# Loading the second token tile from GpSimd's queue, and transposing the first two tiles ahead of the first FFN product

## The chip, the cores and the metric

The kernel runs on one core of a Trainium2 chip. The metric is the device time of one execution in microseconds (us). The engines are named as in the profile: PE is TensorE, ACT is ScalarE, DVE is VectorE, POOL is GpSimd, SP is SyncE, which here only issues DMAs.

## What is computed

The input x has 2048 tokens of 640 features (bf16). It is normalised per token, then goes into two branches: linear attention with 32 heads of 20 features, and a two-layer FFN with 1728 hidden features. The output is x + s * g.

```python
xn = layernorm(x)                       # over the 640 features
q, k, v = split(xn @ wqkv)              # 32 heads
pq, pk = phi(q), phi(k)                 # phi(t) = t+1 if t > 0 else exp(t), plus 1e-6
o = (pq @ (pk.T @ v)) / (pq . sum(pk) + 1e-6)     # per head
s = o @ wo
g = silu(relu(xn @ w1) @ w2)
out = x + s * g
```

## The kernel before

The order of the work is written out by hand. A small recorder (`Sched`) takes each operation with the engine it is to run on, adds the semaphore waits that its reads and writes call for, and emits for each engine its instructions in the order of the calls. So each engine works through its own list in order, and an instruction that waits holds everything behind it on that engine. DMAs stand in the list of the engine that issues them.

Tokens are handled in 16 tiles of 128. The features of a tile are 5 chunks of 128. The FFN's first product and the query product work on groups of four tiles (512 tokens). The change lies in the start, where the first four tiles are brought in:

- `x_load(t)` (L334) loads tile t of x, 128 rows of 1280 bytes, into one of eight slots. `w1_load(i)` (L362) loads one of four column pieces of w1: columns 0 to 383, 384 to 639, 640 to 1151 and 1152 to 1727. `w_load` (L338) loads the key columns of wqkv ("wk"), the query columns ("wq") and others. L368 to L373 issue x0, x1, x2, the second piece of w1 and x3 from SP, and the first piece of w1 from ACT.
- L344 to L350 are POOL's first instructions: constants, among them `ident`, the identity that the transposes need.
- `fill` (L354) runs products of constants on PE into bank 0, whose results nobody reads.
- For tiles 0 to 3, `T_mean(t)` (L418) forms the mean of each token, on DVE or ACT, `center` (L430) subtracts it on DVE, `T_pe` (L435) transposes the chunks on PE into a PSUM bank, and `T_copy` (L440) copies them from there to `xnT`, on ACT or DVE. The division by the standard deviation comes later, in the scales of other operations.
- `H_first(t, fs, ks)` (L578) forms, for tile t alone, the first FFN product of the hidden blocks `fs` over the feature chunks `ks`, each block in a PSUM bank of its own (2 to 6); tile 3's call also evicts the blocks through a ReLU on ACT (`H_ev`). Blocks 0 to 2 need the first piece of w1, 3 and 4 the second.
- `LN_stats` (L392) forms mean and variance for the scales. From L688 on the key products (`K_mm`, L458) alternate with the other hidden blocks (`H_block`, L555); block 5 is the first reader of w1's third piece.

L584 to L626 order the start: nine fillers; tile 0's mean, centring, transposes and copies; 15 products of tile 0; then tile 1's mean, centring, transposes and copies; and so on through tile 3. A call `center(...)` returns a mark, kept as `held`, for which the next weight load waits on SP's queue.

Of the kernel before, what the change touches and what calls it, by code (L numbers as in the profile page):

```python
# [211 lines left out]
def bass_recurrent_scan__linear_attn_block__dense_activation_relu__prompt_kernel(  # L212
# [17 lines left out]
    C = D // P  # L230
# [92 lines left out]
    def dma(E, fn, R=(), W=(), extra=()):  # L323
        i = nds[0]
        nds[0] += 1
        return sc.dma(E, fn, i, R=R, W=W, extra=extra)

    def tok(t):
        return slice(P * t, P * (t + 1))
# [4 lines left out]
    def x_load(t, extra=(), E="SP"):  # L334
        sl = t % XR
        return dma(E, lambda eng: eng.dma_start(xin[:, sl, :], x2[tok(t), :]), W=[("xin", sl)], extra=extra)  # L336

    def w_load(dst, src, key, extra=(), E="SP"):  # L338
        dma(E, lambda eng: eng.dma_start(dst, src.rearrange("(c p) n -> p c n", p=P)), W=[key], extra=extra)


    cones = nc.const_aps.tensor(1.0, [P, P], bf)
    cwide = nc.const_aps.tensor(1.0, [P, 512], bf)
# [3 lines left out]
                                                fill=1.0, base=0, pattern=[[-1, P]], channel_multiplier=1),  # L347
# [6 lines left out]
    def fill(n, w=512):  # L354
        sc.group("PE", [(lambda eng: eng.matmul(ps[0][:, 0:w], lhsT=cones, rhs=cwide[:, 0:w], start=True, stop=True))
                        for _ in range(n)], W=[("ps", 0)])
# [5 lines left out]
    def w1_load(i, extra=(), E="SP"):  # L362
        w_load(w1_sb[:, :, W1C[i]:W1C[i + 1]], B_w1[:, W1C[i]:W1C[i + 1]], ("w1", i), extra, E)
# [3 lines left out]

    x_load(0)  # L368
    w1_load(0, E="ACT")
    x_load(1)  # L370
    x_load(2)
    w1_load(1)
    x_load(3)  # L373
# [18 lines left out]
    def LN_stats(t):  # L392
        xv = xin[:, t % XR, :]
        for a in range(2):
            sc.op("DVE", lambda eng, a=a: eng.bn_stats(stats[:, t, a, :], xv[:, HN * a:HN * (a + 1)]),  # L395
                  R=[("xin", t % XR)], W=[("stats", t, a)])
        sc.op("DVE", lambda eng: eng.bn_aggr(mv[:, t, :], stats[:, t, :, :].rearrange("p a b -> p (a b)")),
              R=[("stats", t, 0), ("stats", t, 1)], W=[("mv", t)])
        sc.op("POOL", lambda eng: eng.tensor_scalar(out=rsv[:, t:t + 1], in0=mv[:, t, 1:2], scalar1=EPS_LN,
                                                    scalar2=None, op0=ALU.add), R=[("mv", t)], W=[("rsv", t)])  # L400
        sc.op("POOL", lambda eng: eng.tensor_tensor(out=rsy[:, t:t + 1], in0=rsv[:, t:t + 1], in1=mhalf[:, :],
                                                    op=ALU.pow), R=[("rsv", t), ("mhalf",)], W=[("rsy", t)])
# [3 lines left out]
    def xnk(t, cs=range(C)):  # L406
        return [("xn", t, c) for c in cs]
# [10 lines left out]
    def T_mean(t, E="ACT"):  # L418
        if E == "ACT":
            sc.op("ACT", lambda eng: eng.activation(out=ek[:, 0, 0, :], in_=xin[:, t, :], func=ACTF.Copy, scale=1.0 / D,  # L420
                                                    accum_out=mean[:, t:t + 1]),
                  R=[("xin", t)], W=[("mean", t), ("ek_e", 0)])
        else:
            sc.op("DVE", lambda eng: eng.tensor_scalar(out=ek[:, 1, 0, :], in0=xin[:, t, :], scalar1=1.0 / D, scalar2=0.0,  # L424
                                                       op0=ALU.mult, op1=ALU.add, accum_out=mean[:, t:t + 1]),
                  R=[("xin", t)], W=[("mean", t), ("ek_e", 1)])
# [3 lines left out]
    def center(t, c0, c1):  # L430
        return sc.op("DVE", lambda eng: eng.tensor_scalar(
            out=xn[:, t, P * c0:P * c1], in0=xin[:, t, P * c0:P * c1], scalar1=mean[:, t:t + 1], scalar2=None,
            op0=ALU.subtract), R=[("xin", t), ("mean", t)], W=xnk(t, range(c0, c1)))

    def T_pe(t, c0, c1, b):  # L435
        psb = ps[b].bitcast(bf)
        sc.group("PE", [(lambda eng, c=c: eng.transpose(psb[:, P * c:P * (c + 1)], xn[:, t, P * c:P * (c + 1)], ident[:]))  # L437
                        for c in range(c0, c1)], R=xnk(t, range(c0, c1)) + [("ident",)], W=[("ps", b)])

    def T_copy(E, t, c0, c1, b):  # L440
        out = xnT[:, c0:c1, tok(t)]
        src = ps[b].bitcast(bf)[:, P * c0:P * c1].rearrange("p (c q) -> p c q", c=c1 - c0)
        if E == "ACT":
            sc.op("ACT", lambda eng: eng.activation(out=out, in_=src, func=ACTF.Copy), R=[("ps", b)],  # L444
                  W=xtk(t, range(c0, c1)))
        else:
            sc.op("DVE", lambda eng: eng.tensor_copy(out, src), R=[("ps", b)], W=xtk(t, range(c0, c1)))

    def xtk(t, cs=range(C)):
        return [("xnT", t, c) for c in cs]  # L450
# [93 lines left out]
    def H_mm(j, f, b, lo=0, hi=512, ks=range(C)):  # L544
        return sc.group("PE", [(lambda eng, k=k: eng.matmul(ps[b][:, lo:hi], lhsT=w1_sb[:, k, P * f:P * (f + 1)],  # L545
                                                            rhs=xnT[:, k, 512 * j + lo:512 * j + hi],
                                                            start=(k == 0), stop=(k == C - 1))) for k in ks],
                        R=[("w1", w1_part(f))] + [kk for q in range(lo // P, hi // P) for kk in xtk(4 * j + q, ks)],
                        W=[("ps", b)])

    def H_ev(j, f, b):
        sc.op("ACT", lambda eng: eng.activation(out=hT[:, f, schunk(j)], in_=ps[b], func=ACTF.Relu),  # L552
              R=[("ps", b)], W=[("hT", j, f)])
# [24 lines left out]
    def H_first(t, fs=range(5), ks=range(C)):  # L578
        for f in fs:
            H_mm(0, f, HF[f], P * t, P * t + P, ks)  # L580
            if t == 3:
                H_ev(0, f, HF[f])

    fill(9)  # L584
    T_mean(0, "DVE")
    center(0, 0, 2)
    T_pe(0, 0, 2, 7)
    held = center(0, 2, 5)
    T_pe(0, 2, 5, 1)
    T_copy("ACT", 0, 0, 2, 7)  # L590
    T_copy("DVE", 0, 2, 5, 1)
    w_load(wqk[:, :, D:2 * D], A_wqkv[:, D:2 * D], ("wk",), [held])
    fill(1, 192)
    H_first(0, (0, 1, 2), (0, 1))
    H_first(0, (0, 1, 2), (2, 3, 4))
    T_mean(1, "DVE")
    center(1, 0, 2)
    T_pe(1, 0, 2, 7)
    held = center(1, 2, 5)
    T_pe(1, 2, 5, 1)  # L600
    T_mean(2)
    T_copy("ACT", 1, 0, 2, 7)
    T_copy("DVE", 1, 2, 5, 1)
    w1_load(2, [held])
    x_load(4)
    x_load(5)
# [1 line left out]
    x_load(6)  # L608
    x_load(7)
    w_load(wqk[:, :, 0:D], A_wqkv[:, 0:D], ("wq",))  # L610
    H_first(0, (3, 4))
    T_mean(3)
    center(2, 0, C)
    H_first(1, (0, 1, 2, 3, 4), (0, 1))
    T_pe(2, 0, C, 7)
    T_copy("ACT", 2, 0, C, 7)
    center(3, 0, C)
    H_first(1, (0, 1, 2, 3, 4), (2, 3, 4))
    T_pe(3, 0, C, 1)
    T_copy("ACT", 3, 0, C, 1)  # L620
    LN_stats(0)
    LN_stats(1)
    LN_stats(2)
    LN_stats(3)
    H_first(2)
    H_first(3, (4, 0, 1, 2, 3))  # L626

    def z_split():
# [376 lines left out]
```

## Time and profile before

| | us |
|---|---|
| median of 3 runs | 222.18 (221.74 to 222.76) |
| the profiled execution | 222.18 |
| its span, from the first to the last instruction | 220.3 |
| PE busy | 215.1 (98%) |
| DVE busy | 115.1 (52%) |
| ACT busy | 87.5 (40%) |
| POOL busy | 43.5 (20%) |

The profile is of one execution. Times within it are us from the start of the span. A timeline row has start, duration, engine, line, operation, output<-input, and in brackets the engine's idle time ahead of it and what ended that. Instructions that are next to each other and alike are merged (x15). A row of a DMA issue (SPq, ACTq) is the time of issuing, not of the transfer; the transfer's end is seen where a reader starts, or in the views on DMA, which give the time from issue to landing. A DMA queue's row gives packets, MB, and the time of its packets as a share of all 16 engines'. `reg` stands for several buffers named reg1 to reg7, `psT` for all PSUM banks.

### The profile page before, as it was taken

To read this page: it belongs to the slowest core of one execution; us is meant where nothing else is said; L and a number is where in the kernel's file an instruction comes from. 1 tells how busy PE (TensorE), PEld (TensorE's weight loads), DVE (VectorE), ACT (ScalarE), POOL (GpSimd) and SP (SyncE) were. 2 spreads that over 40 slices of the span, in tenths; PEclk is the share of its full clock that TensorE was granted. 3 is DMA by queue.
4 is the path that set the end of the run, shared out by engine and by line. 5 is a ranking of instruction groups with operands and counts; after the bars stand their busy time and mean duration, and the time that the engine had idled before them with its cause. 6 is when DMAs were issued, how large, how long until landed. Compare 5 with 4: busy or idle time off the path is not lost.

```text
span 220.3 us, 3568 instructions
## 1 busy us (share of the span) xinstructions
PE 215.1 (98%) x1479; PEld 134.3 (61%) x1490; DVE 115.1 (52%) x198; ACT 87.5 (40%) x142; POOL 43.5 (20%) x66
## 2 busy tenths in 40 slices
PE   8899999999999999999999999999999999999994
PEld 2875554555545554444467778767767776777673
DVE  2878856789676999987700006603322222214053
ACT  3677775567656666555321114641021102110300
POOL 2153201269122997700000000000000000000001
PEclk9999999999999999999999999999999999999999
DMA  6995582213012105700069959368110100000002
GB/s 169 365 369 131 129 211 79 60 39 23 0 30 60 33 1 118 168 4 0 0 192 361 276 167 353 112 224 287 63 62 0 60 33 30 31 30 33 30 30 89
DMA packets 28812, 24.51 MB, mean 111 GB/s; under 512 B 11812, under 2 KB 28156, under 8 KB 28796
## 3 DMA queue, kind: packets, MB, share of 16 engines
q1 hardware_dynamic: 27996, 23.70, 37.1%
q10 hardware_dynamic: 800, 0.59, 1.0%
q8 instruction: 11, 0.18, 0.4%
q14 instruction: 5, 0.04, 0.1%
HBM read 15.75 MB, written 5.24 MB: 95 GB/s over the span
## 4 chain that ended last, share of the span: by engine, by line
PE 95%; DMA 2%; DVE 1%; issue 0%; SPq 0%
PE psT L845 26%; PE psT L545 25%; PE psT L891 10%; PE psT L462 10%; PE psT L790 10%; PE psT L530 10%; DMA reg<-in_A_x_dram 2%; PE psT L861 1%; PE psT L567 1%; PE psT L801 1%; PE psT L812 1%; PE psT L648 1%; PE psT L437 1%; DVE ek L424 0%; SPq L336 0%
## 5 line engine op out<-in xcount | busy, mean ns | idle before, releaser
L545 PE MATMUL psT<-reg 128*128 128x512 bf16 (+1 forms) x326 | 60.1, 330 | 0.8 <-ACT reg L444 0.2
L845 PE MATMUL psT<-reg,hT 128*128 128x320 bf16 x416 | 60.1, 299 | 0.0
L845 PEld LDWEIGHTS psT<-reg,hT 128*128 128x128 bf16 x416 | 40.4, 98 | 16.4 <-issue 1.1
L545 PEld LDWEIGHTS psT<-reg 128*128 128x128 bf16 x335 | 28.6, 98 | 25.9 <-issue 0.4
L913 DVE TENSOR_TENSOR reg<-psT,reg 128x640 bf16<-128x640 f32 x15 | 12.4, 825 | 54.0 <-PE psT L891 53.9
L552 ACT ACTIVATE hT<-psT 128x512 bf16<-128x512 f32 x52 | 30.7, 600 | 16.1 <-PE psT L545 16.0
L879 ACT ACTIVATE reg<-psT 128x640 bf16<-128x640 f32 (+1 forms) x13 | 8.4, 661 | 44.3 <-PE psT L845 24.9
L898 POOL TENSOR_TENSOR reg<-reg 128x256 bf16<-128x256 bf16 x1 | 0.7, 670 | 124.4 <-DVE reg L906 124.4
L530 PE MATMUL psT<-reg 128*128 128x512 bf16 x98 | 24.4, 379 | 0.1
L462 PE MATMUL psT<-reg 128*128 128x320 bf16 x160 | 24.2, 299 | 0.0
L471 POOL TENSOR_TENSOR zacc<-zacc,reg 128x640 f32<-128x640 f32 x16 | 23.7, 1484 | 1.9 <-DVE reg L505 1.0
L891 PE MATMUL psT<-reg,pqT 128*128 128x320 bf16 (+2 forms) x165 | 24.0, 295 | 0.0
L790 PE MATMUL psT<-reg 128*128 128x320 bf16 x160 | 21.9, 299 | 0.0
L462 PEld LDWEIGHTS psT<-reg 128*128 128x128 bf16 x160 | 15.6, 98 | 8.2
L891 PEld LDWEIGHTS psT<-reg,pqT 128*128 128x128 bf16 x165 | 16.0, 98 | 5.8
L790 PEld LDWEIGHTS psT<-reg 128*128 128x128 bf16 x160 | 15.7, 98 | 6.2
L540 DVE SCALAR_TENSOR_TENSOR pqT<-er 128x512 bf16<-128x512 bf16 x20 | 17.1, 854 | 0.7
L530 PEld LDWEIGHTS psT<-reg 128*128 128x128 bf16 x100 | 9.7, 98 | 11.7 <-DVE er L538 0.6
L537 ACT ACTIVATE er<-psT 128x512 bf16<-128x512 f32 x20 | 12.0, 598 | 8.9 <-PE psT L530 8.1
L538 DVE TENSOR_SCALAR er<-psT 128x512 bf16<-128x512 f32 x20 | 13.6, 679 | 3.1 <-ACT er L537 3.1
L505 DVE TENSOR_TENSOR reg<-ek 128x640 bf16<-128x640 bf16 x16 | 13.5, 843 | 1.5 <-ACT ek L496 1.0
L395 DVE BATCH_NORM_STATS2 stats<-reg 128x6 f32<-128x320 bf16 x32 | 13.9, 477 | 0.1
(63 smaller groups left out, 134.9 us busy)
## 6 DMA issues: line engine op xcount, KB each, us to landing
reg<-in_A_x_dram SPq DMA_DIRECT2D x16, 160.0 KB, 3.7
rscr<-rden SPq DMA_DIRECT2D x4, 640.0 KB, 11.1
reg<-rscr SPq DMA_DIRECT2D x5, 512.0 KB, 6.4
reg<-in_A_x_dram SPq DMA_DIRECT2D x4, 640.0 KB, 6.9
out_dram<-reg SPq DMA_DIRECT2D x15, 160.0 KB, 1.8
reg<-in_A_wqkv_dram SPq DMA_DIRECT2D x2, 800.0 KB, 7.3
reg<-in_B_w_dram SPq DMA_DIRECT2D x1, 1120.0 KB, 5.9
reg<-in_B_w_dram SPq DMA_DIRECT2D x1, 960.0 KB, 9.6
```

The costliest lines, as they stand in the source:

```text
L395: sc.op("DVE", lambda eng, a=a: eng.bn_stats(stats[:, t, a, :], xv[:, HN * a:HN * (a + 1)]), R=[("xin", t % XR)], W=[("stats", t, a)])
L462: fns.append(lambda eng, a=a, k=k: eng.matmul(ps[b + a][:, 0:HN], lhsT=xnT[:, k, tok(t)], rhs=wqk[:, k, D + HN * a:D + HN * (a + 1)], star ...
L471: sc.op("POOL", lambda eng: eng.tensor_tensor(out=zacc[:, :], in0=zacc[:, :], in1=pk[:, t, :], op=ALU.add), R=[("zacc",), ("pk", t)], W=[( ...
L505: sc.op("DVE", lambda eng: eng.tensor_tensor(out=pk[:, t, :], in0=e_, in1=r_, op=ALU.add), R=[("ek_e", es), ("ek_r", es)], W=[("pk", t)])
L530: sc.group("PE", [(lambda eng, k=k: eng.matmul(ps[b], lhsT=wqk[:, k, P * f:P * (f + 1)], rhs=rhs(k), start=(k == 0), stop=(k == C - 1))) f ...
L538: sc.op("DVE", lambda eng: eng.tensor_scalar(out=r_, in0=ps[b], scalar1=0.0, scalar2=1e-6, op0=ALU.max, op1=ALU.add), R=[("ps", b), ("er_e ...
L540: sc.op("DVE", lambda eng: eng.scalar_tensor_tensor(out=pqT[:, f, schunk(j)], in0=e_, scalar=1.0, in1=r_, op0=ALU.min, op1=ALU.add), R=[(" ...
L545: return sc.group("PE", [(lambda eng, k=k: eng.matmul(ps[b][:, lo:hi], lhsT=w1_sb[:, k, P * f:P * (f + 1)], rhs=xnT[:, k, 512 * j + lo:512 ...
L552: sc.op("ACT", lambda eng: eng.activation(out=hT[:, f, schunk(j)], in_=ps[b], func=ACTF.Relu), R=[("ps", b)], W=[("hT", j, f)])
L790: fns.append(lambda eng, t=t, a=a: eng.matmul(ps[b + a][:, 0:HN], lhsT=xn[:, t, P * k:P * (k + 1)], rhs=pk[:, t, HN * a:HN * (a + 1)], sta ...
L845: sc.group("PE", [(lambda eng, f=f, n=n: eng.matmul(ps[b + n][:, 0:HN], lhsT=hT[:, f, tok(t)], rhs=w2_sb[:, f, HN * n:HN * (n + 1)], start ...
L891: sc.group("PE", [(lambda eng, c=c, pb=pb, lo=lo, hi=hi: eng.matmul(ps[pb][:, 0:hi - lo], lhsT=pqT[:, c, tok(t)], rhs=wf[:, c, lo:hi], sta ...
```

## The change

The load of x1 moves from SP's list to the head of POOL's, ahead of the constants. Tile 1's mean moves from DVE to ACT, and its centring is one instruction, not two. The transposes of tiles 0 and 1 both stand ahead of the first product of tile 0, and the 192-wide filler between them goes. Behind them the products of tiles 0, 1 and 2 are cut by hidden block (0 to 2, then 3 and 4) and no longer by feature chunk for tile 1; tile 2's copy is on DVE, tile 3's stays on ACT; the banks of the transposes change. The third piece of w1, and what stands behind it on SP's list, waits for tile 2's centring and no longer for tile 1's.

```diff
@@ -338,6 +338,8 @@
+    x_load(1, E="POOL")
+
 
     cones = nc.const_aps.tensor(1.0, [P, P], bf)
...
     x_load(0)
     w1_load(0, E="ACT")
-    x_load(1)
     x_load(2)
     w1_load(1)
     x_load(3)
@@ -583,24 +584,24 @@
     fill(9)
     T_mean(0, "DVE")
+    T_mean(1)
     center(0, 0, 2)
     T_pe(0, 0, 2, 7)
     held = center(0, 2, 5)
     T_pe(0, 2, 5, 1)
     T_copy("ACT", 0, 0, 2, 7)
+    center(1, 0, C)
     T_copy("DVE", 0, 2, 5, 1)
+    T_pe(1, 0, 2, 0)
+    T_pe(1, 2, 5, 7)
+    T_copy("ACT", 1, 0, 2, 0)
+    T_copy("DVE", 1, 2, 5, 7)
     w_load(wqk[:, :, D:2 * D], A_wqkv[:, D:2 * D], ("wk",), [held])
-    fill(1, 192)
     H_first(0, (0, 1, 2), (0, 1))
     H_first(0, (0, 1, 2), (2, 3, 4))
-    T_mean(1, "DVE")
-    center(1, 0, 2)
-    T_pe(1, 0, 2, 7)
-    held = center(1, 2, 5)
-    T_pe(1, 2, 5, 1)
     T_mean(2)
-    T_copy("ACT", 1, 0, 2, 7)
-    T_copy("DVE", 1, 2, 5, 1)
+    held = center(2, 0, C)
+    H_first(1, (0, 1, 2))
     w1_load(2, [held])
     x_load(4)
     x_load(5)
@@ -608,21 +609,20 @@
     x_load(6)
     x_load(7)
     w_load(wqk[:, :, 0:D], A_wqkv[:, 0:D], ("wq",))
+    T_pe(2, 0, C, 1)
+    T_mean(3)
     H_first(0, (3, 4))
-    T_mean(3)
-    center(2, 0, C)
-    H_first(1, (0, 1, 2, 3, 4), (0, 1))
-    T_pe(2, 0, C, 7)
-    T_copy("ACT", 2, 0, C, 7)
+    T_copy("DVE", 2, 0, C, 1)
     center(3, 0, C)
-    H_first(1, (0, 1, 2, 3, 4), (2, 3, 4))
-    T_pe(3, 0, C, 1)
-    T_copy("ACT", 3, 0, C, 1)
+    H_first(1, (3, 4))
+    H_first(2, (0, 1, 2))
+    T_pe(3, 0, C, 0)
+    T_copy("ACT", 3, 0, C, 0)
     LN_stats(0)
     LN_stats(1)
     LN_stats(2)
     LN_stats(3)
-    H_first(2)
+    H_first(2, (3, 4))
     H_first(3, (4, 0, 1, 2, 3))
```

## The prediction

> **What bounds the kernel now.** The page's head and its chain come first.
>
> ```profile
> span 220.3 us, 3568 instructions
> PE 95%; DMA 2%; DVE 1%; issue 0%; SPq 0%
> ```
>
> The chain that ended last is TensorE for 95% of the span. So the question is when TensorE begins to run without a break. The chain in order of time, cut to its first 16 us, shows that (start, duration, what):
>
> ```profile
> 1.25 4.61 DMA reg<-in_A_x_dram
> 5.86 0.02 issue
> 5.88 0.84 DVE ek L424 x2
> 6.72 0.02 issue
> 6.75 0.30 DVE reg L431
> 7.04 0.05 issue
> 7.09 0.57 PE psT L437 x5
> 7.66 1.12 PE psT L545 x20
> 8.78 0.28 PE psT L437 x5
> 9.06 0.84 PE psT L545 x15
> 9.89 0.28 PE psT L437 x5
> 10.17 2.79 PE psT L545 x50
> 12.96 2.72 PE psT L462 x20
> ```
>
> It starts at the load of x1, which lands at 5.86. Mean, centring and transposes of tile 1 follow, and from 7.09 every piece is TensorE. The first key product (K, L462) starts at 12.96. Any delay or gain up to there reaches the end; behind it the chain is TensorE's. The early timeline shows what runs before x1 is there:
>
> ```profile
> 0.78 0.20 POOL L344 MEMSET onesM<- 128x128 bf16 x1 [0.29 <-POOLq L990]
> 0.79 1.35 SPq L336 DMA_DIRECT2D reg<-in_A_x_dram  x3
> 1.36 0.29 POOL L346 TENSOR_SCALAR_AFFINE_SELECT ident<-ident 128x128 bf16<-128x128 bf16 x1 [0.23 <-POOL ident L345]
> 3.52 0.82 DVE L424 TENSOR_SCALAR_CACHE_REDUCE ek<-reg 128x640 bf16<-128x640 bf16 x1 [3.52 <-DMA reg<-in_A_x_dram]
> 4.38 0.52 DVE L431 TENSOR_SCALAR reg<-reg,mean 128x256 bf16<-128x256 bf16 x2
> 4.73 0.57 PE L437 MATMUL psT<-ident,reg 128*128 128x128 bf16 x5
> 5.05 0.38 ACT L444 ACTIVATE reg<-psT 128x256 bf16<-128x256 bf16 x1 [2.48 <-PE psT L437]
> 5.33 0.36 DVE L447 COPY reg<-psT 128x384 bf16<-128x384 bf16 x1 [0.43 <-PE psT L437]
> 5.54 1.00 PE L545 MATMUL psT<-reg 128*128 128x128 bf16 x15 [0.16 <-ACT reg L444]
> 6.33 0.74 ACT L420 ACTIVATE ek<-reg 128x640 bf16<-128x640 bf16 x1 [0.90 <-DMA reg<-in_A_x_dram]
> 6.98 0.19 ACT L420 ACTIVATION_READ_ACCUMULATOR ek<-reg 128x1 f32 x1
> 8.45 0.19 ACT L420 ACTIVATION_READ_ACCUMULATOR ek<-reg 128x1 f32 x1
> 8.67 0.39 DVE L431 TENSOR_SCALAR reg<-reg,mean 128x640 bf16<-128x640 bf16 x1 [0.32 <-ACT ek L420]
> 10.21 0.70 ACT L444 ACTIVATE reg<-psT 128x640 bf16<-128x640 bf16 x1 [0.41 <-PE psT L437]
> ```
>
> x0 lands at 3.5, and tile 0's first 15 FFN products fill 5.54 to 6.54, **in the shadow of the wait for x1**. x2 lands at about 6.31 (ScalarE's mean starts on it at 6.33). Everything turns on why x1 takes 4.6 us where x0 took 2.7. The DMA queues' packets in three stretches (1.8 to 2.6, 3.2 to 4.25, 4.25 to 5.25; q1 is SP's, q10 ScalarE's) answer it; the last four rows are issues, with size and us to landing (the first piece of w1, x0, wk, the third piece of w1):
>
> ```profile
> q1 hardware_dynamic: 95, 0.12, 80.8%
> q10 hardware_dynamic: 6, 0.00, 7.9%
> ```
> ```profile
> q10 hardware_dynamic: 310, 0.24, 78.4%
> ```
> ```profile
> DMA packets 432, 0.38 MB, mean 384 GB/s; under 512 B 23, under 2 KB 432, under 8 KB 432
> q10 hardware_dynamic: 288, 0.21, 62.1%
> q1 hardware_dynamic: 144, 0.18, 47.5%
> ```
> ```profile
> reg<-in_B_w_dram ACTq DMA_DIRECT2D x1, 480.0 KB, 4.6
> reg<-in_A_x_dram SPq DMA_DIRECT2D x1, 160.0 KB, 2.7
> reg<-in_A_wqkv_dram SPq DMA_DIRECT2D x1, 800.0 KB, 6.1
> reg<-in_B_w_dram SPq DMA_DIRECT2D x1, 640.0 KB, 5.5
> ```
>
> First x0 alone; then, from 3.2 to 4.25, **only the first piece of w1**, although SP had issued x1 at about 1.25; x1's rows come when that piece is through, around 5. The engines did not switch to a waiting queue in the middle of that transfer. x1's issue time is not what made it late.
>
> **The change part by part.** L below is when x1 lands in the changed kernel.
>
> *The load.* It leaves SP's queue and becomes GpSimd's first instruction behind the barrier, at about 0.78 instead of 1.25. No row here has a load issued by GpSimd, so L is bounded by neighbours: 0.78 + 2.7 = 3.5 if it goes as x0 did, 0.78 + 6.1 = 6.9 if as wk did. I take 5.86, its present landing, since q10's rows are what it must pass: a third queue is ready at best beside x0, while w1's piece has been issued at 0.79 and is already moving on some engines before 2.6.
>
> The Trainium skill ("DMA: Bandwidth & Descriptors", section "Issuing engines are not separate DMA queues") speaks against the change: loads issued by GpSimd, ScalarE and SP run on the same 16 engines, and another issuer saves only issue time. By it, L stays near 5.9, and the trace so far agrees: x1's issue at 1.25 was 3 us ahead of its rows. The same page (section "Anatomy of one DMA") fits a GpSimd load at 2.0 us plus bytes over 436 GB/s; an estimate by it is 2.4 us, L near 3.2, if nothing were in its way, and no run here shows that yet.
>
> GpSimd's masks stand behind the load. The identity is done at 1.65 and first used at 4.73, so 3 us of issuing are hidden; beyond that tile 0 itself would be late. SP loses one issue (1.35 / 3 = 0.45 us), so x2, the second piece of w1 and x3 are issued that much earlier. That buys nothing: their bytes still wait behind the first piece of w1, and x1's bytes are ahead or among them. wk stays tied to tile 0's centring (4.90) and lands at 4.92 + 6.1 = 11.0, before 12.96. The third piece of w1 now waits for tile 2's centring, not tile 1's; that ends near 9.1, so landing is near 14.6, and its first reader stands behind K, at 15.68 now. Hidden, with over 1 us in hand, and the same wait holds x4 to x7 and wq, read later.
>
> *The path from x1 to tile 1's transposes.* Mean on ScalarE (6.33 to 7.17, 0.84), wake-up 0.02, hand-over to DVE 0.03 (8.64 to 8.67), centring in one piece 0.39, hand-over to TensorE 0.05: **L + 1.33**, against 7.09 - 5.86 = 1.23. This adds waits. The mean heads ScalarE's stream, so tile 0's ScalarE copy is held; tile 1's centring on DVE waits for it and holds tile 0's DVE copy; tile 1's transposes on TensorE stand ahead of all products. So **nothing of tile 0's FFN runs before x1**: the 15 products from 5.54 come out of the shadow. The 192-wide filler (0.25) goes, and was in the gap anyway.
>
> *TensorE from there to K.* Tile 1's five transposes 0.57; then 30 products, 5 transposes, 35, 5, 35: 110 instructions of 2.79 / 50 = 0.056, 6.14. The copies of tiles 0 and 1 end under the transposes and the first 15 products (0.84), as does tile 2's DVE copy under 20 products. Tile 3's does not: after its transposes only ten products (0.56) stand ahead of those that need the copy. The copy starts 0.04 after the transposes (10.17 to 10.21), takes 0.70, TensorE resumes 0.11 later (5.43 to 5.54), and the restart costs 0.16 (15 products took 1.00, not 0.84): 1.01 - 0.56 = **0.45 of new stall**. Before, 25 products (1.40) covered it.
>
> *Sum.* K starts at L + 1.33 + 0.57 + 6.14 + 0.45 = **L + 8.49**. Now it is 12.96, so break-even is L = 4.47. With L = 5.86, K starts at 14.35, 1.39 late: 0.84 for the uncovered products, 0.45 for the copy, 0.10 for the slower path. What follows is TensorE's, and the DVE and ScalarE work that feeds it moves along. The profiled execution took 222.18 us (span 220.3, 1.88 around it), equal to the median of the runs shown: 222.18 + 1.39 = **223.6 us**.
>
> **The rivals.**
> 1. *x1 passes the weights.* GpSimd's queue gets its turn right behind x0 on every engine, or is served beside w1's piece. For it: it is a queue of its own, x0's rows ended late on some engines, and the early stretch moves little. Against: all 16 engines must do so, as the last one sets L, and w1's piece was issued first. For L below 4.0, K is set by tile 0's centring (4.90, then 0.03 + 0.39 + 0.05 to 5.37, then 0.57 + 6.14 + 0.45: 12.53) or by x2 if it still lands at 6.31 (tile 2's transposes at 6.31 + 1.33 = 7.64, 0.44 with the restart, 75 x 0.056 = 4.19, 0.45: 12.72). Not slower: **221.7 to 222.0**, and it decides from L = 4.47 down. Even without the copy stall the gain stays under 0.9.
> 2. *x1 shares with the weights.* L between 4.5 and 5.6: K 0 to 1.1 late, **222.2 to 223.3**. Against it: the stretch with 310 packets of q10 and none of q1.
> 3. *Later still.* x1 comes behind x2 as well, or GpSimd is slow to issue. L = 6.31 gives K at 14.80 and 224.0, still the forecast's kind; the bound 6.9 gives 15.4, **224.6**.
>
> **How the numbers follow.** Forecast (L 5.6 to 6.4, 223.3 to 224.1): 0.50. Rival 1: 0.27. Rival 2: 0.12. Rival 3: 0.11. The range takes in rival 1 but its lowest end and stops inside rival 3: **221.7 to 224.3**; the forecast's own range is 223.3 to 224.1. A measurement here can tell about 0.5%, 1.11 us, from no change. Slower by more needs L over 5.58: the forecast and rival 3 less a little for my terms, 0.58. Faster by more is beyond rival 1's floor, left for terms unseen: 0.03. Within: 0.39.
>
> **What would show it.** Right: ScalarE's first mean starts near 5.9; the first FFN product stands behind ten transposes, after 7; a TensorE gap of about 0.45 behind tile 3's transposes, released by ScalarE's copy; K near 14.3; GpSimd's rows among the packets only when q10's are nearly through. Wrong: a mean starting before 4.5, or GpSimd's packets while q10's first ones run; then K stands before 13. Wrong in another place: identity ready after 4.7, or a wait of K for wk.

## The result and the profile after

The changed kernel is slower: a median of 226.06 us (225.06 to 226.77, 6 runs) against 222.05 us (221.74 to 223.17, 6 runs), ratio 1.0171, 95% interval 1.0149 to 1.0194. The forecast was 223.6 with a range to 224.3: right in sign, and less than half of the loss. Executions of one kernel that has a long gap on TensorE differ by up to 4.5 us here; the ratios leave out those more than 1.5% above their kernel's fastest.

The profiled execution took 225.97 us. From its page: the span, the granted clock in 40 slices (before it was 9 throughout) and the new queue, q0, which is GpSimd's (packets, MB, share of 16 engines).

```profile
span 224.1 us, 3576 instructions
PEclk9699999999999999999999999999999999999999
q0 software_dynamic: 48, 0.16, 0.2%
```

The second slice, from 5.6 to 11.2 us, shows a clock of 0.6, which nothing in the forecast had. The chain in order of time, to the first key product (K); pieces called "issue", of 0.14 us at most, are left out here and below:

```profile
1.30 5.01 DMA reg<-in_A_x_dram
6.33 0.84 ACT ek L421 x2
7.19 0.40 DVE reg L432
7.64 0.71 PE psT L438 x5
8.35 2.90 PE psT L546 x30
11.26 0.28 PE psT L438 x5
11.54 1.95 PE psT L546 x35
13.49 0.29 PE psT L438 x5
13.81 0.71 ACT reg L445
14.57 1.57 PE psT L546 x25
16.14 2.73 PE psT L463 x20
```

K starts at 16.14 where it stood at 12.96: 3.18 of the 3.8 us by which the span grew. Tile 1's transposes start at 7.64, exactly L + 1.33 with L = 6.31. ScalarE's copy of tile 3 stands in the chain, as foreseen, though TensorE itself is idle there for 0.24 us only. What wasn't foreseen is the line of 30 products: 2.90 us, 0.097 each, where the next 35 take 1.95, 0.056 each. Three stretches of 1 us show why (busy time and instructions of PE, PEld, DVE, ACT and POOL, then granted clock, DMA share and GB/s):

```profile
6.00:7.00 1.00, 0.00 (x0) 0.00 (x0) 0.00 (x0) 0.67 (x2) 0.00 (x0) 1.00 1.10 368
8.00:9.00 1.00, 1.00 (x13) 1.00 (x11) 0.36 (x1) 0.93 (x3) 0.00 (x0) 0.50 1.01 346
9.00:10.00 1.00, 1.00 (x12) 1.00 (x11) 0.39 (x1) 0.97 (x4) 0.00 (x0) 0.50 0.09 28
```

TensorE is idle from 5.16 to 7.64, and behind that gap it runs **at half its clock** (granted 0.5 from about 7.4 to 10.8): 12 or 13 products in 1 us, not the 22 of the stretch from 11 to 12.

The remaining 0.6 us come later: tile 7's key product waits for the DMA transpose of its tokens (L454, issued from SP). Two lines of the chain further on:

```profile
28.99 4.50 DMA reg<-reg
...
33.62 1.52 PE psT L463 x10
```

It stands 17.48 behind K; in the kernel before it starts at 29.86, 16.90 behind. The transfer took 4.50 us here, 2.8 there.

On the DMA engines the forecast's picture held. The queues' packets from 3.2 to 4.25, then from 4.25 to 5.25, and the issue with its time to landing:

```profile
q10 hardware_dynamic: 390, 0.30, 93.4%
```
```profile
q1 hardware_dynamic: 150, 0.16, 45.4%
q10 hardware_dynamic: 186, 0.13, 39.1%
q0 software_dynamic: 24, 0.11, 26.2%
```
```profile
reg<-in_A_x_dram POOLq DMA_DIRECT2D x1, 160.0 KB, 5.0
```

GpSimd's rows wait until w1's piece is nearly through, as SP's had. GpSimd's own timeline tells where the issue went:

```profile
1.30 0.77 POOL L336 DMA_DIRECT2D reg<-in_A_x_dram  x1 [0.81 <-POOLq L990]
2.69 0.29 POOL L348 TENSOR_SCALAR_AFFINE_SELECT ident<-ident 128x128 bf16<-128x128 bf16 x1 [0.24 <-POOL ident L347]
```

Though first on its engine, the load begins at 1.30, later than SP's issue of x1 at 1.25, and the identity is done 1.3 us later than before, still ahead of its first use (4.59).

### The profile page after: what moved, and what is told of

It is laid out like the page before. It is cut to its first block, busy times and chain, and to the rows that moved or that the text cites. A ratio compares the mean times of both kernels' runs of the same rounds, so it can differ in the third digit from the quotient of the medians.

```text
span 224.1 us, 3576 instructions
## 1 busy us (share of the span) xinstructions
PE 216.9 (97%) x1489; PEld 135.6 (61%) x1489; DVE 114.4 (51%) x196; ACT 87.3 (39%) x143; POOL 44.3 (20%) x67
## 4 chain that ended last, share of the span: by engine, by line
PE 88%; DMA 4%; DVE 3%; POOL 1%; ACT 1%; issue 1%; SPq 0%; POOLq 0%
PE psT L845 25%; PE psT L546 22%; PE psT L891 10%; PE psT L790 10%; PE psT L531 10%; PE psT L463 7%; DMA reg<-in_A_x_dram 2%; DMA reg<-reg 2%; PE psT L861 1%; DVE stats L396 1%; POOL rsy L402 1%; PE psT L568 1%; PE psT L801 1%; PE psT L812 1%; PE psT L438 1%
## 5 line engine op out<-in xcount | busy, mean ns | idle before, releaser
L546 PE MATMUL psT<-reg 128*128 128x512 bf16 (+1 forms) x335 | 63.1, 338 | 0.2 <-ACT reg L445 0.2
L546 PEld LDWEIGHTS psT<-reg 128*128 128x128 bf16 x335 | 29.8, 102 | 26.0 <-issue 0.4
L531 PE MATMUL psT<-reg 128*128 128x512 bf16 x100 | 24.9, 379 | 0.0
L463 PEld LDWEIGHTS psT<-reg 128*128 128x128 bf16 x160 | 15.5, 98 | 8.9 <-ACT ek L497 0.9
L790 PEld LDWEIGHTS psT<-reg 128*128 128x128 bf16 x160 | 15.7, 98 | 6.2
L531 PEld LDWEIGHTS psT<-reg 128*128 128x128 bf16 x100 | 9.7, 98 | 11.6 <-DVE er L539 0.6
## 6 DMA issues: line engine op xcount, KB each, us to landing
rscr<-rden SPq DMA_DIRECT2D x4, 640.0 KB, 10.8
```

Of the source, the lines that this page charges most:

```text
L463: fns.append(lambda eng, a=a, k=k: eng.matmul(ps[b + a][:, 0:HN], lhsT=xnT[:, k, tok(t)], rhs=wqk[:, k, D + HN * a:D + HN * (a + 1)], star ...
L531: sc.group("PE", [(lambda eng, k=k: eng.matmul(ps[b], lhsT=wqk[:, k, P * f:P * (f + 1)], rhs=rhs(k), start=(k == 0), stop=(k == C - 1))) f ...
L790: fns.append(lambda eng, t=t, a=a: eng.matmul(ps[b + a][:, 0:HN], lhsT=xn[:, t, P * k:P * (k + 1)], rhs=pk[:, t, HN * a:HN * (a + 1)], sta ...
```

## The experiments

Each is compared with runs of the kernel before on the same chip (medians 221.85 to 222.09).

**The order alone.** x1 goes back to SP's queue.

```diff
-    x_load(1, E="POOL")
...
     w1_load(0, E="ACT")
+    x_load(1)
     x_load(2)
```

> The changed kernel with x1 loaded from SP between x0 and x2 as before; only the new order is left. My theory: the order alone costs most, because nothing covers the wait for x1. With x1 at 5.86 tile 1's transposes start at 7.19, TensorE idles 2.0 us ahead of them, and K starts at 14.35 if TensorE keeps its full clock (about 223.5 us), at about 15.6 if the clock is halved behind the gap as in the changed kernel's stretch from 7.6 to 10.4 (about 225). Rival (the software queue itself is what costs): within 0.5 us of the kernel before, 222 to 222.6.

Measured: 225.21 us (222.74 to 227.23, 10 runs), ratio 1.0121 (1.0088 to 1.0154). The order without the software queue costs 1.2%; the rival is out. Much of the wide spread goes with the clock: four of the ten executions have a mean clock of 0.991 or 0.992 and took 225.50 to 225.95. The profiled execution was the fastest, 222.74: x1 landed early, at 5.34, TensorE kept its full clock behind 1.55 us of idling, and K started at 13.68. So one program stands on both sides of the clock's drop (its second profile, below, shows the half speed).

**The load alone.** The old order, x1 from GpSimd.

```diff
+    x_load(1, E="POOL")
...
-    x_load(1)
     x_load(2)
```

> The kernel before with x1 loaded from GpSimd as its first instruction; the order is the old one. My theory: x1 lands at 6.3 instead of 5.86, the 15 products of tile 0 stand in the gap as before, no idle stretch over 1.1 us, the clock stays, and only the 0.45 us of the later landing is paid: 222.3 to 222.8 us. Rival (the software queue itself is what costs): 224 us or more.

Measured: 222.70 us, ratio 1.0032 (1.0014 to 1.0049). As foreseen, the load by itself is a small loss; not as foreseen, x1 lands at 5.93 in the profile and not at 6.3. There tile 0's 15 products fill the gap, the clock stays at 1.0 and K starts at 13.03.

**Fillers in the gap.** Ten products of constants on TensorE, whose results nobody reads.

```diff
+    fill(10)
     T_pe(1, 0, 2, 0)
```

> The changed kernel with ten 512-wide fillers (2.2 us) on TensorE between the transposes of tile 0 and of tile 1. They do no work; they only keep TensorE busy. My theory: the granted clock stays at 1.0 from 7 to 11, the 30 products take 1.7 us instead of 2.9, K starts at about 14.8 instead of 16.1 and the time is 224.2 to 224.8 us. Rival (the products were slow for another reason, for instance the first reading of w1's piece): K stays at 16.1 and the time at 226.

Measured: 224.07 us (223.64 to 224.42), ratio 1.0094 (1.0076 to 1.0112), against 1.0171 without fillers. The same 30 products, K, and one of the stretches:

```profile
7.76 1.68 PE psT L546 x30
...
14.31 2.72 PE psT L463 x20
```
```profile
8.00:9.00 1.00, 1.00 (x22) 1.00 (x20) 0.39 (x2) 0.97 (x4) 0.00 (x0) 1.00 1.01 370
```

They take 1.68, not 2.90; with L = 5.96, K starts at 14.31. The fillers end at 7.48, 0.19 after tile 1's transposes could have begun. **Idle work on TensorE is worth 0.8%**, so the slow products came from the gap and not from w1's first reading.

**w1's first piece in five parts.** One DMA for each feature chunk, 8 rows for each DMA engine. Each product waits for the part that it reads (a line not shown).

```diff
-    w1_load(0, E="ACT")
+    for c in range(C):
+        dma("ACT", lambda eng, c=c: eng.dma_start(w1_sb[:, c, 0:3 * P], B_w1[P * c:P * (c + 1), 0:3 * P]),
+            W=[("w1", 0, c)])
```

> The changed kernel with the first piece of w1 loaded in five parts, one for each feature chunk (8 rows for each DMA engine instead of 40), from ScalarE as before. My theory (a DMA engine does not leave a transfer that it has begun, and x1 is late because it stands behind 40 rows): GpSimd's rows get their turn after one or two parts, x1 lands between 3.9 and 5, there is no long gap and the clock stays; K starts between 12.6 and 13.5, 222 to 222.8 us. Rival (GpSimd's queue is slow by itself): x1 still lands at 6 or later, and the time is 225 us or more.

Measured: 225.74 us, ratio 1.0185 (1.0155 to 1.0215): the time missed my number by far. GpSimd's queue from 3.2 to 4.25, and then a part of the chain:

```profile
q0 software_dynamic: 32, 0.13, 45.0%
```
```profile
1.30 4.22 DMA reg<-in_A_x_dram
...
7.79 2.56 PE psT L548 x24
```

The mechanism is there: with short transfers the engines take turns, and 32 of x1's 48 packets move in the stretch in which none did. But x2, issued earlier, now goes by as well (SP's queue moves 194 packets by 3.2, 50 more than x0 has), 16 of x1's packets come after 4.25, and it lands at 5.53, between theory (5 at most) and rival (6). TensorE then idled for 1.54 us, and its clock fell here too: 0.107 for each of 24 products.

**GpSimd's load with little beside it.** w1's piece and SP's loads behind x0 wait for x1.

```diff
-    x_load(1, E="POOL")
+    x1_done = x_load(1, E="POOL")
...
-    w1_load(0, E="ACT")
-    x_load(2)
+    w1_load(0, [x1_done], E="ACT")
+    x_load(2, [x1_done])
```

> The changed kernel with the first piece of w1 (ScalarE) and SP's loads behind x0 held until x1 has landed, so that GpSimd's load has only x0 beside it. Read for one number, x1's landing; the rest is late by design. My theory (its lateness in the changed kernel is the queue on the DMA engines): issued from 1.3, it lands between 3.7 and 4.8. Rival (GpSimd's way of issuing is slow by itself): 5.5 or later.

Measured (226.32 us, one execution): issued at 1.30, landed at 4.14, as the theory had it. From 2.6 to 3.2 and from 3.2 to 4.25:

```profile
q0 software_dynamic: 19, 0.09, 68.7%
```
```profile
q0 software_dynamic: 29, 0.07, 17.1%
```

Its first packets are 1.3 us or more behind the issue. By then w1's piece, in the changed kernel, has begun (79 packets of q10 between 2.6 and 3.2). So even with only x0 beside it GpSimd's load lands at 4.1, 2.84 us after its start, where x0 from SP took 2.7 in the kernel before: it loses the race and isn't slow in itself. The clock fell in this execution too, behind two idle stretches of 1.88 and 0.70 us.

**x1 ahead of the weights.** From ScalarE's queue, in front of w1's first piece; the new order stays.

```diff
-    x_load(1, E="POOL")
...
+    x_load(1, E="ACT")
     w1_load(0, E="ACT")
```

> The changed kernel's order, with x1 loaded from ScalarE ahead of the first piece of w1 instead of from GpSimd. My theory (whoever stands first on the engines lands first, and the new order needs x1 before about 4.5): x1 lands between 3.8 and 4.4, w1's piece near 5.9, tile 1's transposes start near 5.4, the gap on TensorE stays under 1 us and the clock at 1.0; K starts between 12.5 and 13.1, 221.7 to 222.3 us. Rival (the new order is slower wherever x1 lands): 223.5 or more.

Measured: 222.15 us, ratio 1.0011 (0.9999 to 1.0023), against 1.0121 for the same order with x1 behind the weights. The ScalarE mean starts at 4.08 in the profile, so x1 landed near 4.06. **The order isn't slow wherever x1 lands; it is slow because x1 lands late.** Nor is it a gain yet. The profiled execution was the slowest of the eleven, 225.30 us, and shows what is left to go wrong: w1's piece landed at 7.32 and not near 5.9. Lines of its chain and a stretch:

```profile
1.23 6.09 DMA reg<-in_B_w_dram
...
7.37 2.76 PE psT L545 x30
```
```profile
9.00:10.00 1.00, 1.00 (x12) 1.00 (x11) 0.00 (x0) 0.00 (x0) 0.00 (x0) 0.50 0.99 287
```

TensorE idled for only 1.16 us ahead of those products (and 0.29 shortly before), and its clock still fell: not at once, but from about 8.1 to 11.5.

**The same, with 25 products behind tile 3's transposes.**

```diff
     H_first(1, (3, 4))
-    H_first(2, (0, 1, 2))
     T_pe(3, 0, C, 0)
...
-    H_first(2, (3, 4))
+    H_first(2)
```

> As the run with x1 ahead on ScalarE's queue, and in addition tile 2's first three products blocks moved behind tile 3's transposes, so that 25 products cover tile 3's copy as in the kernel before. My theory: the copy's stall of 0.4 us goes, K starts between 12.1 and 12.7, 221.3 to 221.9 us, about 0.4 below its sibling. Rival (tile 3's transposes then wait as long for its centring): no difference from its sibling.

Measured: 221.64 us, ratio 0.9995 (0.9978 to 1.0012); the median is 0.5 below its sibling's, as the theory has it, but the interval holds no difference from the kernel before. K starts at 12.38, and tile 3's copy is not in the chain.

**Fillers, and 25 products behind tile 3's transposes.** The last edit on top of the fillers.

> The changed kernel with the ten fillers and with 25 products, not 10, behind tile 3's transposes. It prices the copy's stall with the clock held up. My theory: 0.40 us below the run with the fillers alone, about 223.7 us, K at 13.9. Rival (the stall moves to tile 3's centring): as the run with fillers, 224.1.

Measured: 223.54 us (223.21 to 223.75), ratio 1.0072 (1.0057 to 1.0087), 0.53 us below the fillers alone by the medians. In the two profiles the way from tile 1's transposes to K takes 6.83 with 10 products (7.48 to 14.31) and 6.42 with 25 (7.82 to 14.24). The copy's stall was priced at 0.45 and is worth about that. In this profile TensorE is busy from 0.83 to K without a gap.

**The old order with x1 ahead.**

```diff
+    x_load(1, E="ACT")
     w1_load(0, E="ACT")
-    x_load(1)
```

> The kernel before, its order unchanged, with x1 loaded from ScalarE ahead of the first piece of w1. My theory: x1 lands near 4 and w1's piece near 5.9, so tile 0's first products move from 5.54 to about 6 and tile 1's transposes come right behind them, from about 6.9; K starts at 12.7 to 12.9, 221.6 to 222.0 us, about 0.2 below the kernel before. Rival (an early x1 needs the new order to be of use): no difference, 222.0 or more.

Measured: 222.36 us, ratio 1.0026 (1.0013 to 1.0038): slower, a miss. K's first product starts at 12.72 (12.80 before), so little was gained; and the chain then leaves TensorE:

```profile
7.63 6.32 DMA reg<-in_A_x_dram
13.98 0.90 DVE stats L395 x2
...
25.74 4.22 DMA reg<-reg
30.10 1.52 PE psT L462 x10
```

x4 lands at 13.95; the statistics of tiles 4 to 7 on DVE and GpSimd follow, then tile 7's DMA transpose, 4.22 us, then its key product. This is **a second chain, close behind TensorE's**.

**A bank of its own for tile 1.** As the run with 25 products and x1 ahead, and the second part of tile 1's transposes goes to a bank that is free until later.

```diff
-    T_pe(1, 2, 5, 7)
+    T_pe(1, 2, 5, 6)
...
-    T_copy("DVE", 1, 2, 5, 7)
+    T_copy("DVE", 1, 2, 5, 6)
```

> As the run with x1 ahead and 25 products behind tile 3's transposes, with the second part of tile 1's transposes in a bank of its own, so that it doesn't wait for ScalarE's copy of tile 0 (5.43 to 5.89 in that run's chain). My theory: the first product starts 0.2 to 0.3 us earlier, K at 12.1 to 12.3 instead of 12.38, 221.3 to 221.6 us, faster than the kernel before. Rival (w1's piece, landing near 5.9, is what the first product waits for): as its sibling, 221.6.

Measured: 221.64 us (221.03 to 222.84, 12 runs), ratio 0.9983 (0.9968 to 0.9998): faster than the kernel before by 0.2%, just clear of none. K is as early as the theory had it, but the median is its sibling's, which is the rival's number. The chain:

```profile
12.20 2.73 PE psT L462 x20
...
25.05 4.50 DMA reg<-reg
29.69 1.52 PE psT L462 x10
```

K starts 0.76 early, and tile 7's key product 0.17 (29.86 before): the second chain takes back 0.6 in this execution.

**The changed kernel once more**, unaltered, for a second profile.

> The changed kernel once more, unaltered, for a second profile. My theory: x1 lands between 5.9 and 6.4 again, the clock is halved behind the gap for about 2.7 us again, and K starts between 15.7 and 16.2; the wait of tile 7's key product for its transpose (0.6 us in the first profile) is chance and absent or smaller. Rival (that wait follows from the late start): again 0.5 us or more.

Measured (one execution): 224.30 us. x1 lands at 6.27, as the theory said, but the clock did *not* fall, against it:

```profile
7.60 0.45 PE psT L438 x5
8.05 1.68 PE psT L546 x30
...
14.60 2.72 PE psT L463 x20
```

So the drop is not certain, even behind 2.24 us of idling. Tile 7's key product waited again: it starts at 32.05, 17.45 behind K, 0.55 more than in the kernel before, and its transpose, issued at 27.47, took 4.4 us. On that point the rival's 0.5 is met; what the long transposes have in common is told further down.

**The order alone once more.**

> The run with the new order alone once more, unaltered, for a second profile, since its executions lie between 222.7 and 227.2 us. My theory: the spread is the clock behind the gap; if this execution takes 224 us or more, its profile shows a granted clock of 0.5 in some of the stretches from 7 to 12, and if it takes 223 or less, 1.0. Rival (the spread is from the loads): a time of 224 or more with the clock at 1.0 and x1 later than 6.

Measured (one execution): 224.64 us. x1 landed at 5.90, and TensorE idled for 1.83 us ahead of tile 1's transposes. The products' line in the chain, and a stretch:

```profile
7.94 2.76 PE psT L545 x30
```
```profile
8.00:9.00 1.00, 1.00 (x12) 1.00 (x10) 0.55 (x2) 0.97 (x4) 0.00 (x0) 1.00 1.03 364
```

12 products in 1 us: half speed again. The column of the granted clock says 1.00, not the 0.5 that I expected; but the page of this profile has no row for the clock at all, so that 1.00 stands for a missing record. (In the kernel before, the stretches from 1 to 4 us read 1.00 as well, while the nine fillers there take 3.98 us, 0.44 each; the ten in the gap, in the run with fillers, take 2.18.) The pace of the products is the record to trust here; a mean clock of 1.0 over a run doesn't prove that the clock was whole.

## Why the prediction was wrong

**The bound and the DMA engines: right.** x1 was late because of what it stood behind. From GpSimd it landed at 6.31, 6.27 and 5.93 (the changed kernel twice, the load alone), from SP at 5.86, 5.34 and 5.90 (the kernel before, the order alone twice); placed ahead of the weights it landed near 4.06, and weights in five parts let it by in part, at 5.53. The Trainium skill ("DMA: Bandwidth & Descriptors", section "Issuing engines are not separate DMA queues"), as the prediction cites it, is borne out: another issuer did not bring the bytes sooner. L was taken as 5.86, with 5.6 to 6.4 as the forecast's bounds: 0.45 of the miss, inside them. "At about 0.78 instead of 1.25" was wrong: the load begins at 1.30.

**The path to tile 1's transposes: right.** L + 1.33, to the hundredth.

**"TensorE from there to K": the step that failed.** It priced 110 instructions at 0.056, the pace of a TensorE that had just been busy, and the removal of the 15 covered products at their own 0.84. It didn't ask what a gap of over 2 us does to the instructions behind it, though before the longest early gap had been 0.55. At full clock the step was good: 7.16 forecast, 7.00 in the second profile (7.60 to 14.60), which puts K at L + 8.33 where the forecast had L + 8.49. In the first profile it took 8.50: the 30 products 2.90 instead of 1.68, the five transposes 0.71 instead of 0.45, together **1.5 us from the clock**. The fillers show the cause: same loads, same order, and the time falls by 0.8%; and the second profile has the same products behind the same loads at 1.68.

The sum of the first profile, term by term: landing 0.45, slower path 0.10, uncovered products and copy 1.13 (forecast 1.29), clock 1.50; together 3.18 at K.

**"What follows is TensorE's": not quite.** 0.6 us came between K and tile 7's key product, at which the chain passes through DVE, GpSimd and a DMA transpose. The slack there was about 1.2 us: in the kernel before the transpose was issued at 25.82, took 2.8 and was read at 29.86. That the same transfer takes 2.8 in one execution and 4.5 in another was not in the forecast. It isn't the late start alone: runs with K at 12.20 and at 16.14 waited, runs with K at 12.38 and at 15.58 did not. What goes with a long one stands in the DMA view of its time, here of the changed kernel from 28.99 to 33.49:

```profile
q8 instruction: 1, 0.02, 2.0%
reg<-reg SPq DMA_TRANSPOSE x1, 4.5
```

One packet of a queue that the profile's page calls "instruction" moves among the 16 DMA engines' work, for about 1.4 us (2.0% of 16 engines in 4.5 us). The 14 profiles hold 42 transposes of tiles 5 to 7. Six have such a packet within them, and these took 4.0 to 4.5: tile 7's in five runs (both profiles of the changed kernel, GpSimd's load with little beside it, the old order with x1 ahead, the bank of its own) and tile 6's in the run with fillers. The other 36 have none and took 2.7 to 3.0. No run moves that packet, so this is a coincidence read from all traces and not a test; how often it meets the changed kernel beyond its two profiles isn't known.

**The copy of tile 3: right**, 0.45 forecast, 0.41 in the profiles and 0.53 by the medians with the clock held.

**Rival 1**, x1 passing the weights, was the sound half of the idea: it happens if the load stands ahead of them, not if it comes by another queue. It was priced 221.7 to 222.0; with x1 truly ahead the order took 222.15, and 221.64 with the copy covered.

The Trainium skill ("TensorE: Matmul & The Clock Gate", section "Part 1: The HAM clock gate (the "warmup" mystery)") describes a monitor that halves the array's clock after an idle window of some 3.4 us, counted freely and not from the kernel's start. The half speed, its stretch of 3.4 us (7.4 to 10.8 in the changed kernel, 8.1 to 11.5 with x1 ahead) and its luck from execution to execution agree with that. The length of the gap does not: here idling of 2.48, 1.83, 1.54 and 1.16 us (the changed kernel, the order alone once more, the five parts, x1 ahead) was followed by half speed, 2.24 and 1.55 (the changed kernel once more, the order alone) were not. By these numbers a gap a third as long as that window is a risk, and its length alone doesn't decide; what does is open.

## What to carry to other kernels

Before you remove work from the shadow of a wait on TensorE, price the gap that it leaves not only by its length but by the pace behind it: gaps of 1.2 to 2.5 us cost up to 1.5 us more, in some executions and not in others, and cheap fillers showed it at once. A load that is late because of the bytes ahead of it isn't helped by another queue; put it ahead. Cutting what is ahead into shorter transfers brought it 0.8 us sooner here and gained no time. And when the first chain is shortened, read the next one (here from x4 to tile 7's transpose) before counting the gain.

## What had not been expected of the hardware

- GpSimd's load occupied the engine for 0.77 us, and its first packets moved at least 1.3 us behind its start; x0's, issued by SP at 0.79, moved from 1.8.
- Its 160 KB went in 48 packets, those of x0 from SP in 144 (95 from 1.8 to 2.6, 49 from 2.6 to 3.2).
- The granted clock read 1.00 in an execution whose products ran at half speed; its profile holds no record of the clock.
- A DMA transpose of 2.7 to 3.0 us took 4.0 to 4.5 whenever a packet of the instruction queue q8 moved within it.
